# One core, a fused attention and feed-forward kernel: attention inputs stored as whole blocks, the first loads reordered, and two pools moved

## The chip, the cores and the metric

The kernel runs on one core of a Trainium2 chip. The metric is device time in microseconds (us), as the median over runs.

Engines are named as the profile names them. PE is the matmul engine, PEld its weight loads, DVE the vector engine, ACT the scalar (activation) engine, and POOL the GpSimd engine. SP is the engine that issues most transfers here; "SPq" is its queue of instructions. A "DMA share" is the mean busy share of the core's 16 DMA engines.

## The reference, cut to what matters

```python
xn = _layernorm(x)                      # x: 1 x 2048 x 1024, bf16
return x + A(xn) + B(xn)

# B: two gated feed-forward steps
h  = gelu(_layernorm(xn) @ w1)          # 1024 -> 1024
hs = shifted_quarters(h) @ w2           # four column groups shifted by rows
x1 = xn + hs
B  = x1 + gelu(_layernorm(x1) @ w3) @ w4   # 1024 -> 3584 -> 1024

# A: attention over segments of 32 rows, 32 heads of 128, 8 memory rows
for s in segments:
    h = concat([mem, xs]);  q, k, v = h @ Wq, h @ Wk, h @ Wv
    o = softmax(mask(q @ k.T)) @ v @ Wo
    mem = o[:8];  out = o[8:]
```

On PE the kernel does this in five stages:

1. **start and w1**: norms of x, transposes, the w1 matmuls; 
2. **w2**; 
3. **w3** (and w4); 
4. **V**: V = xT·Wv for all rows, stored to memory; 
5. **attention**: Q and K projections, scores, outputs and Wo for five blocks of rows.

## The kernel before: the parts that matter

The V phase has eight head groups `hg`. Each makes 4 x 4 PSUM tiles, evicts them alternately on ACT and DVE into a buffer `Vs` (three of them), and stores each full `Vs` from SP. After head group 1, POOL issues sixteen stores of xT, which the attention blocks read back later.

```python
vsp = vctx.enter_context(tc.tile_pool(name="vsp", bufs=3, side="right"))
...
for hg in range(8):
    ...                                     # loads of Wv and Wo, from POOL
    for m4 in range(4):
        Vs = vsp.tile([P, 4, 512], BF16, tag="Vs")
        for j in range(4):
            ps = psum.tile([P, 512], F32, tag="mm", bufs=4)
            for k in range(KT):
                nc.tensor.matmul(ps[:], xT[:, m4 * 4 + j, k, :], wv[:, k, :], ...)   # L569
            if j % 2 == 0:
                nc.scalar.copy(Vs[:, j, :], ps[:])                                   # L571
            else:
                nc.vector.tensor_copy(Vs[:, j, :], ps[:])                            # L573
        nc.sync.dma_start(V_d[...], Vs[:])                                           # L574
    if hg == 1:
        for t in pns:
            nc.gpsimd.memset(t[:], 0.0)
        for n in range(NT):                                                          # NT = 16
            nc.gpsimd.dma_start(xT_d[:, :, n * P:(n + 1) * P], xT[:, n])             # L579
    if hg == 6:
        first_w = [wtile(), wtile()]        # Wq, Wk of the first head group
        ...
vctx.close()
...
qkv = actx.enter_context(tc.tile_pool(name="aqkv", bufs=2))    # QT, KT, V: where vsp was
```

A later block reads its rows of xT in four or five strided pieces, and the rows of memory are copied in beside them:

```python
hTb = early.tile([P, KT, nt, 104], BF16, tag="hTb")
for i in range(nt):
    nc.gpsimd.dma_start(hTb[:, :, i, 0:96], xT_d[:, :, a + 96 * i:a + 96 * (i + 1)])
nc.vector.tensor_copy(hTb[:, :, :, 96:99], MZ[...])
```

The start loads x in tiles of 128 rows and w1 in two halves of 1 MB. DVE does the statistics, the norms and half of the casts of the first tile.

```python
load_x(0)
for c in range(2):
    nc.sync.dma_start(w1_sb[:, :, c * 512:(c + 1) * 512], w1_v[:, :, c * 512:(c + 1) * 512])
    load_x(c + 1)
for n in range(3, 7):
    load_x(n)
...                                         # in norm1(n), n < 4: a quarter of w2
norm_stats(0)
t0 = xn2T_tile()
xn2 = norm2(0, t0, 0)
norm_stats(1, 0)                            # first half of the statistics of tile 1
transposes(xn2, t0, 0, 0)
transposes(xn2, t0, 0, 1, on_dve=True)
norm_stats(1, 1)
```

The intermediate `h3T` of the w3 stage comes from the pool `p3big`, and the last stores of the output are issued by POOL (`nc.gpsimd.dma_start(out_v[...], ot[:])`).

## Time and profile before

Three runs gave 1540.99 us (1538.52 to 1541.14). The profiled run took 1540.65 us, with a span of 1538.9 us. Each stage starts where its first matmul appears in the view of one line's instructions. The lengths follow by subtraction.

| stage of before | us |
|---|---|
| start and w1 (until the first w2 matmul) | 75.4 |
| w2 | 55.3 |
| w3 and w4 | 413.7 |
| V | 227.1 |
| attention, to its last output matmul | 761.0 |
| from there to the end of the span | 6.4 |

The first view is the page's part 1: engine, busy us, share of the span, number of instructions. PE is the limit, so a change helps only where PE idles or runs at half clock, or after PE's last matmul.

```profile
PE 1516.0 (99%) x9870; PEld 810.3 (53%) x9870; DVE 522.2 (34%) x1094; ACT 506.1 (33%) x1154; POOL 192.5 (13%) x272
```

Next the view of waits for PE. Each line says who waited at which line of the kernel, for whom, then us in all, how often, and the longest.

```profile
PE ps L282 <- DVE xn L261: 7.0, 1, 7.0
PE ps L569 <- ACT Vs L571: 4.3, 1, 4.3
PE ps L514 <- ACT h3T L515: 1.1, 1, 1.1
PE ps L638 <- DMA wt<-in_A_Wq_dram: 1.0, 2, 0.7
PE psO L677 <- DMA PT<-Pn: 0.9, 1, 0.9
PE ps L291 <- DVE xnk L270: 0.8, 1, 0.8
PE psS L653 <- ACT KT L644: 0.6, 1, 0.6
...
```

The largest wait after the start sits in the V phase, on ACT. But ACT itself waited, as the view of its waits from 560 to 600 us shows first. The view of three windows then gives, for each stretch: its length, the busy time of each engine, the granted clock, the DMA share and GB/s.

```profile
ACT Vs L571 <- DMA V_scratch<-Vs: 17.5, 2, 10.7
...
```

```profile
core 0: us, PE busy (x) PEld busy (x) DVE busy (x) ACT busy (x) POOL busy (x), PEclk, DMA share, GB/s
545.00:570.00 25.00, 25.00 (x117) 11.34 (x116) 5.09 (x8) 4.00 (x7) 13.86 (x18) 1.00 0.93 324
570.00:600.00 30.00, 25.73 (x113) 11.27 (x112) 4.75 (x7) 3.90 (x7) 7.25 (x9) 0.95 0.98 260
600.00:630.00 30.00, 30.00 (x139) 13.56 (x138) 5.53 (x8) 5.26 (x9) 1.75 (x2) 0.99 0.60 206
...
```

So ACT could not evict because all three `Vs` were still being stored, and the DMA engines were full (0.98) when it happened. The trace's clock record also shows that PE ran at half clock from 597.16 us for 3.41 us, right after the stall; the granted clocks of 0.95 and 0.99 in the last two windows are this.

The timeline has, per line: start, length, engine, line, operation, and in brackets the idle time before it and what ended that.

At the change from V to attention (771.5 us), the timelines show ACT's first QT eviction after 4.89 us of idling. It waited for the last `Vs` store to land.

```profile
775.42 0.33 SPq L623 DMA_DIRECT2D V<-V_scratch  x1
...
776.62 0.95 SPq L723 DMA_DIRECT2D wt<-in_A_Wq_dram  x2
...
```

```profile
775.44 1.31 ACT L646 ACTIVATE QT<-ps 128x403 bf16<-128x403 f32 x3 [4.89 <-DMA V_scratch<-Vs]
...
```

### The profile page before, as it was taken

The page shows a single profiled execution, that of the slowest core. Times are in us where ns is not written, and L with a number is a line of the kernel's source. Part 1 is how long each engine was busy: PE and PEld are TensorE (multiplying, and loading weights), DVE is VectorE, ACT ScalarE, POOL GpSimd, SP SyncE. Part 2 cuts the span into 40 slices and gives each one's busy share as a digit, 9 for nine tenths or more (in the row PEclk, how much of TensorE's full clock was granted, in tenths as well). Part 3 has the DMA queues.
Part 4 walks back from the last instruction along what each step waited for, and adds up shares of the span by engine and source line. Part 5 has one row for each costly group of instructions (what it writes and reads, how often), then busy time and mean ns, then how long its engine had stood idle before and what let it go on. Part 6 is the DMA issues. An engine that isn't in the chain of part 4 may idle for free. (4 is left out here: it accounts for less than half of the span.)

```text
span 1538.9 us, 24379 instructions
## 1 busy us (share of the span) xinstructions
PE 1516.0 (99%) x9870; PEld 810.3 (53%) x9870; DVE 522.2 (34%) x1094; ACT 506.1 (33%) x1154; POOL 192.5 (13%) x272
## 2 busy tenths in 40 slices
PE   7999999999999998999999999999999999999998
PEld 7844444444444443444456645664665555445554
DVE  8284010000200111122135623651564266416641
ACT  5533203103012011111146614650663266326620
POOL 5232020221211241010000011001000200010001
PEclk9999999999999999999999999999999999999999
DMA  7689543452353898542489956992997389728611
GB/s 253 182 224 309 199 154 121 144 185 83 128 168 83 215 275 260 187 130 69 137 218 250 242 133 166 251 234 71 237 239 196 102 218 228 185 75 207 174 45 50
DMA packets 288445, 270.32 MB, mean 176 GB/s; under 512 B 137307, under 2 KB 255216, under 8 KB 288328
## 3 DMA queue, kind: packets, MB, share of 16 engines
q1 hardware_dynamic: 264936, 185.52, 45.5%
q0 software_dynamic: 23392, 83.19, 16.6%
q8 instruction: 79, 1.29, 0.4%
q14 instruction: 38, 0.31, 0.1%
HBM read 190.73 MB, written 46.73 MB: 154 GB/s over the span
## 5 line engine op out<-in xcount | busy, mean ns | idle before, releaser
L638 PE MATMUL ps<-hTb,wt 128*128 128x396 bf16 (+3 forms) x2560 | 509.9, 343 | 1.0 <-DMA wt<-in_A_Wq_dram 1.0
L638 PEld LDWEIGHTS <-wt 128*128 128x128 bf16 x2560 | 233.9, 97 | 168.3 <-DMA wt<-in_A_Wq_dram 1.8
L569 PE MATMUL ps<-wt,xT 128*128 128x512 bf16 x1024 | 223.0, 381 | 4.3 <-ACT Vs L571 4.3
L696 PE MATMUL pso<-wo_sb,oX 128*128 128x512 bf16 x1024 | 225.1, 379 | 0.0
L514 PE MATMUL ps<-xn3T,w_sb 128*128 128x512 bf16 x896 | 195.9, 379 | 1.1 <-ACT h3T L515 1.1
L539 PE MATMUL ps<-w_sb,h3T 128*128 128x512 bf16 x896 | 195.7, 379 | 0.0
L569 PEld LDWEIGHTS <-xT 128*128 128x128 bf16 x1024 | 100.6, 98 | 126.6 <-issue 6.8
L515 ACT ACTIVATE h3T<-ps 128x512 bf16<-128x512 f32 x112 | 66.5, 597 | 292.0 <-PE ps L514 289.0
L696 PEld LDWEIGHTS <-oX 128*128 128x128 bf16 x1024 | 98.8, 98 | 115.4
L644 ACT CAST KT<-ps 128x396 bf16<-128x396 f32 (+3 forms) x160 | 82.0, 513 | 221.8 <-PE ps L638 219.9
L514 PEld LDWEIGHTS <-w_sb 128*128 128x128 bf16 x896 | 86.7, 98 | 104.0 <-issue 1.3
L539 PEld LDWEIGHTS <-h3T 128*128 128x128 bf16 x896 | 86.8, 98 | 102.8
L659 DVE TENSOR_REDUCE sums<-sm 99x4 f32<-99x396 f32 (+2 forms) x176 | 97.5, 554 | 113.2 <-ACT sm L657 113.2
L655 DVE TENSOR_TENSOR sm<-psS,c_mask_reg_sb 99x396 f32<-99x396 f32 x160 | 91.1, 570 | 88.9 <-PE psS L653 88.4
L657 ACT ACTIVATE sm<-sm 99x396 f32<-99x396 f32 (+2 forms) x176 | 92.7, 527 | 76.3 <-DVE sm L655 75.7
L571 ACT CAST Vs<-ps 128x512 bf16<-128x512 f32 x64 | 37.2, 585 | 239.6 <-PE ps L569 161.4
L646 ACT ACTIVATE QT<-ps 128x396 bf16<-128x396 f32 (+3 forms) x160 | 83.8, 525 | 74.9 <-PE ps L638 50.2
L573 DVE CAST Vs<-ps 128x512 bf16<-128x512 f32 x64 | 44.1, 691 | 183.0 <-PE ps L569 159.3
L665 DVE TENSOR_TENSOR Pn<-sm,rs 99x396 bf16<-99x396 f32 (+2 forms) x176 | 98.9, 562 | 6.2 <-DMA PT<-Pn 0.2
L540 DVE TENSOR_TENSOR R<-ps,R 128x512 f32<-128x512 f32 x32 | 22.1, 691 | 231.8 <-PE ps L539 226.2
L703 POOL DMA_DIRECT2D out_dram<-ot x32 | 17.5, 546 | 588.1 <-DVE ot L702 582.2
L678 ACT CAST oX<-psO 128x384 bf16<-128x384 f32 (+1 forms) x176 | 82.5, 469 | 9.0 <-PE psO L677 8.5
(114 smaller groups left out, 980.8 us busy)
## 6 DMA issues: line engine op xcount, KB each, us to landing
wt<-in_A_Wq_dram SPq DMA_DIRECT2D x78, 512.0 KB
wt<-in_A_Wk_dram SPq DMA_DIRECT2D x78, 512.0 KB
wt<-in_A_Wv_dram POOLq DMA_DIRECT2D x24, 1024.0 KB, 7.0
V_scratch<-Vs SPq DMA_DIRECT2D x32, 512.0 KB
V<-V_scratch SPq DMA_DIRECT2D x32, 384.0 KB
w_sb<-in_B_w_dram SPq DMA_DIRECT2D x9, 1024.0 KB
R_scratch<-x POOLq DMA_DIRECT2D x16, 512.0 KB, 4.3
R<-R_scratch SPq DMA_DIRECT2D x16, 512.0 KB
```

The source lines that it names most:

```text
L514: nc.tensor.matmul(ps[:].rearrange("p (n t) -> p n t", t=P), w3_sb[:, k, f * P:(f + 1) * P], xn3T[tb][:, :, k, :], start=(k == 0), stop=(k ...
L539: nc.tensor.matmul(ps[:], h3T[:, f, j * P:(j + 1) * P], w4_sb[:, f, ch * 512:(ch + 1) * 512], start=(f == 0), stop=(f == FT - 1))
L569: nc.tensor.matmul(ps[:], xT[:, m4 * 4 + j, k, :], wv[:, k, :], start=(k == 0), stop=(k == KT - 1))
L638: nc.tensor.matmul(ps[:, :nb] if flat else ps[:, :nb].rearrange("p (t c) -> p t c", t=nt), w[:, k, hh * P:(hh + 1) * P], B["rhs"](k), star ...
L644: nc.scalar.copy(o, i)
L646: nc.scalar.mul(o, i, scale)
L655: nc.vector.tensor_tensor(sm[:T, :, :T], S3, t["mask"][:].unsqueeze(1).to_broadcast((T, 4, T)), op=ALU.add)
L657: nc.scalar.activation(e[:T, :, :T], sm[:T, :, :T], ACTF.Exp, scale=LN2)
L659: nc.vector.tensor_reduce(ss, e[:T, :, :T], axis=AX.X, op=ALU.add)
L665: nc.vector.tensor_tensor(Pn[:T, :, :T], e[:T, :, :T], rs[:T, :].unsqueeze(2).to_broadcast((T, 4, T)), op=ALU.mult)
L678: nc.scalar.copy(oX[:, hs_, at:at + nt], O3[:, :, 0:nt])
L696: nc.tensor.matmul(self.ps[:], self.oX[:, h, self.gl * P:(self.gl + 1) * P], wo_sb[:, h, self.cc], start=(h == 0), stop=(h == H - 1))
```

## The change

Its intent, part by part:

- **Whole blocks.** In head groups 1 to 4, DVE copies the rows of one attention block, memory rows included, into a tile `hTs`. One contiguous store per block (0.85 to 1.06 MB) replaces the burst of sixteen, and one contiguous load later replaces four or five strided ones.
- **Start.** x's second tile is loaded ahead of w1, w2 is loaded at once, thirteen matmuls on zeros keep PE busy so that its clock opens, the gelu function table is loaded by a dummy activation, and half of tile 1's statistics go into DVE's wait for POOL.
- **Pools.** `h3T` gets a pool of its own; the QT, KT and V pool moves to the other side, away from `vsp`.
- **Small things.** The second head group's Wq is loaded during the V phase, the exp table is loaded there too, and the last two output stores are issued by SP.

```diff
-    xT_d = tc.dram_tile([P, KT, S], BF16, name="xT_scratch")
+    hT_d = {b: tc.dram_tile([P, KT * c], BF16, ...) for b, c in ((1, 416), (2, 416), (3, 432), (4, 520))}
@@ start
                     load_x(0)
+                    load_x(1)
                     for c in range(2):
                         nc.sync.dma_start(w1_sb[:, :, c * 512:(c + 1) * 512], ...)
-                        load_x(c + 1)
-                    for n in range(3, 7):
+                        load_x(c + 2)
+                    for n in range(4, 7):
                         load_x(n)
+                    for i in range(4):
+                        nc.sync.dma_start(w2_sb[:, 2 * i:2 * i + 2, :], ...)
+                    wz = big.tile([P, 512], BF16)
+                    nc.vector.memset(wz[:], 0.0)
+                    gtab = big.tile([P, 1], F32)
+                    nc.scalar.activation(gtab[:], ones_f[:], ACTF.Gelu_apprx_tanh)
+                    ps = psum.tile([P, 512], F32, tag="mm", bufs=4, name="warm")
+                    for i in range(13):
+                        nc.tensor.matmul(ps[:], wz[:, :P], wz[:], start=(i == 0), stop=(i == 12))
                     norm_stats(0)
+                    norm_stats(1, 0)
                     t0 = xn2T_tile()
                     xn2 = norm2(0, t0, 0)
-                    norm_stats(1, 0)
@@ w3 stage
+                h3T = p3.enter_context(tc.tile_pool(name="p3h", bufs=1)).tile([P, FT, 512], BF16)
                 big = p3.enter_context(tc.tile_pool(name="p3big", bufs=1))
...
-                h3T = big.tile([P, FT, 512], BF16)
@@ V phase
+                            if (hg, m4, j) == (7, 3, 2):
+                                nc.scalar.activation(etab[:], ps[:, 0:1], ACTF.Exp, scale=0.0)
...
-                    for n in range(NT):
-                        nc.gpsimd.dma_start(xT_d[:, :, n * P:(n + 1) * P], xT[:, n])
+                if 1 <= hg < 5:
+                    b, (tl, nb) = hg, tiles_of(hg)
...
+                    hTs = abig.tile([P, KT, 432 if b == 3 else 104 * len(tl)], BF16, tag="oX", ...)
+                    nc.gpsimd.memset(hTs[:], 0.0)
+                    fill(hTs, tl, lambda j, b=b: xT[:, j])
+                    nc.gpsimd.dma_start(hT_d[b][:], hTs[:].rearrange("p k c -> p (k c)"))
...
+                if hg == 7:
+                    second_w = [wtile()]
+                    nc.sync.dma_start(second_w[0][:], Wq_v[:, :, 512:1024])
@@ attention
-        qkv = actx.enter_context(tc.tile_pool(name="aqkv", bufs=2))
+        qkv = actx.enter_context(tc.tile_pool(name="aqkv", bufs=2, side="right"))
...                                          # blocks: one load of hTb from hT_d[b]
-                    nc.gpsimd.dma_start(out_v[:, self.gi, self.cc], ot[:])
+                    (nc.sync if self.last else nc.gpsimd).dma_start(out_v[:, self.gi, self.cc], ot[:])
```

More of the change, by code (lines that the diff above doesn't have):

```diff
@@ L112 @@
     xn_v = xn_d.rearrange("(n p) d -> p n d", p=P)
-    xT_d = tc.dram_tile([P, KT, S], BF16, name="xT_scratch")
+    hT_d = {b: tc.dram_tile([P, KT * c], BF16, name=f"hT{b}_scratch") for b, c in ((1, 416), (2, 416), (3, 432), (4, 520))}
     V_d = tc.dram_tile([S, H * DH], BF16, name="V_scratch")
@@ L172, in fill @@
         for t in tl:
-            a = t["tok"]
+            a = 96 * t["gi"]
             end = a + t["ntok"]
@@ L177, in fill @@
                 w = min(P - o, end - a)
-                d = t["c0"] + a - t["tok"]
+                d = t["c0"] + a - 96 * t["gi"]
                 nc.vector.tensor_copy(hTb[:, :, d:d + w], x_of(j)[:, :, o:o + w])
@@ L228 @@
                     load_x(0)
+                    load_x(1)
                     for c in range(2):
                         nc.sync.dma_start(w1_sb[:, :, c * 512:(c + 1) * 512], w1_v[:, :, c * 512:(c + 1) * 512])
-                        load_x(c + 1)
-                    for n in range(3, 7):
+                        load_x(c + 2)
+                    for n in range(4, 7):
                         load_x(n)
+                    for i in range(4):
+                        nc.sync.dma_start(w2_sb[:, 2 * i:2 * i + 2, :], w2_v[:, 2 * i:2 * i + 2, :])
                     stats = {}
@@ L272, in norm1 @@
                         load_x(n + 7)
-                        if n < 4:
-                            nc.sync.dma_start(w2_sb[:, 2 * n:2 * n + 2, :], w2_v[:, 2 * n:2 * n + 2, :])
-                        elif n in (12, 15):
+                        if n in (12, 15):
                             load_w3()
@@ L554 @@
             oT_m = abig.tile([P, H, NQ + 1], BF16)
+            etab = abig.tile([P, 1], F32)
             wo_sb = abig.tile([P, H, D], BF16)
@@ L577 @@
                         nc.gpsimd.memset(t[:], 0.0)
-                    for n in range(NT):
-                        nc.gpsimd.dma_start(xT_d[:, :, n * P:(n + 1) * P], xT[:, n])
+                if 1 <= hg < 5:
+                    b, (tl, nb) = hg, tiles_of(hg)
+                    if b != 3:
+                        for t in tl:
+                            t["c0"] = 104 * t["i"]
+                    hTs = abig.tile([P, KT, 432 if b == 3 else 104 * len(tl)], BF16, tag="oX", name=f"hTs{b}")
+                    nc.gpsimd.memset(hTs[:], 0.0)
+                    fill(hTs, tl, lambda j, b=b: xT[:, j])
+                    nc.gpsimd.dma_start(hT_d[b][:], hTs[:].rearrange("p k c -> p (k c)"))
                 if hg == 6:
@@ L597, in block_setup @@
             ntok = sum(t["ntok"] for t in tl)
-            a = 384 * b
             if b == 0:
                 hTb, rhs = hTb0, lambda k: hTb0[:, k, :nb]
-            elif b == 3:
-                hTb = early.tile([P, KT, 432], BF16, tag="hTb")
-                for t in tl:
-                    nc.gpsimd.dma_start(hTb[:, :, t["c0"]:t["c0"] + t["ntok"]], xT_d[:, :, 96 * t["gi"]:96 * t["gi"] + t["ntok"]])
-                    d = t["c0"] + t["ntok"]
-                    nc.vector.tensor_copy(hTb[:, :, d:d + t["nm"]], MZ[:, :, t["r0"]:t["r0"] + t["nm"]])
-                rhs = lambda k: hTb[:, k, :nb]
             else:
                 nt = len(tl)
-                hTb = early.tile([P, KT, nt, 104], BF16, tag="hTb")
-                r0 = tl[0]["r0"]
-                for i in range(nt):
-                    nc.gpsimd.dma_start(hTb[:, :, i, 0:96], xT_d[:, :, a + 96 * i:a + 96 * (i + 1)])
-                nc.vector.tensor_copy(hTb[:, :, :, 96:99], MZ[:, :, r0:r0 + 3 * nt].rearrange("p k (t r) -> p k t r", t=nt))
-                rhs = lambda k: hTb[:, k, :, 0:99]
-                for i, t in enumerate(tl):
-                    t["c0"] = 104 * i
+                hTb = early.tile([P, KT, 432 if b == 3 else 104 * nt], BF16, tag="hTb")
+                nc.gpsimd.dma_start(hTb[:].rearrange("p k c -> p (k c)"), hT_d[b][:])
+                if b == 3:
+                    rhs = lambda k: hTb[:, k, :nb]
+                else:
+                    rhs = lambda k: hTb[:, k, :].rearrange("p (t c) -> p t c", t=nt)[:, :, 0:99]
+                    for t in tl:
+                        t["c0"] = 104 * t["i"]
             return dict(b=b, tiles=tl, nb=nb, ntok=ntok, rhs=rhs, cols=nb if b in (0, 3) else 104 * len(tl))
@@ L686, in __init__ @@
                 self.oX, self.gi, self.gl, self.cc, self.ps = oX, gi, gl, slice(ch * 512, (ch + 1) * 512), None
-                self.late = False
+                self.late = self.last = False
             def piece(self, hg):
@@ L714, in load_some, with stage_loads @@
                 loads.pop(0)()
-        def stage_loads(Bs, hg, ready=None):
+        def stage_loads(Bs, hg, ready=()):
             cs_ = slice(hg * 512, (hg + 1) * 512)
-            wq, wk = ready or (wtile(), wtile())
+            ws = [(w, None) for w in ready]
+            ws += [(wtile(), src) for src in (Wq_v, Wk_v)[len(ready):]]
+            (wq, _), (wk, _) = ws
             Vs = [qkv.tile([P, len(B["tiles"]), 512], BF16, tag="V", bufs=3, name=f"V{B['b']}") for B in Bs]
-            for w, src in () if ready else ((wq, Wq_v), (wk, Wk_v)):
+            for w, src in ws[len(ready):]:
                 for k0 in (0, 4):
@@ L761 @@
                 if hg < 7:
-                    ahead = stage_loads(Bs, hg + 1)
+                    ahead = stage_loads(Bs, hg + 1, second_w if (gi_, hg) == (0, 0) else ())
                 if hg == 7 and gi_ + 1 < len(groups):
@@ L800 @@
             o.late = True
+        for o in rest[-2:]:
+            o.last = True
         for p in range(6):
```

## The prediction

> **What bounds the kernel now.** PE: the table of busy time gives it 1516.0 of 1538.9 us, in dense runs of matmuls. Only PE's idle time and time at half clock can be won. The view of PE's waits lists about 17 us: 7.0 us at the start (first transpose, waiting for DVE), 4.27 us once in the V phase (waiting for ACT's eviction into Vs), 1.07 us at the start of the w3 stage (ACT's h3T), 0.34 + 0.65 us for the second Wq load, 0.91 us for a PT transpose, 0.81 us at 18 us for a normalized tile, the rest 0.2 to 0.6 each. After PE's last matmul (about 1532.9 us in the timeline) come 6 us of tail.
>
> **Change by change.**
>
> 1. *xT stores.* In the V phase POOL stores xT in 16 pieces of 256 KB (559 to 580 us); the DMA share of 570 to 600 us is 0.98, against 0.52 to 0.60 later. Stores of Vs land late, ACT and DVE wait about 10 us for Vs buffers (until 596.5), and PE stalls 4.27 us. The granted clock then is 0.5 for 3.41 us: another 1.7 us. (The Trainium skill, "TensorE: Matmul & The Clock Gate", section "The HAM clock gate", says an idle window of about 3.4 us halves the clock; the trace agrees.) After: four contiguous stores of 0.85 to 1.06 MB, 27 us apart; I estimate a DMA share of 0.7. Stall and half clock go: **-6.0 us**. DVE pays with 9 to 12 copies per block, 0.18 to 0.36 us each by hTb's copies in the trace: bursts of about 2.6 us against one PSUM bank of four filled per 1.73 us. That barely fits: +0.3 us.
>
> 2. *Start.* PE's first 40 matmuls take about 112 ns each, later ones 65. Thirteen zero matmuls in the idle 7 us should leave the clock full at 7.0 us. The gelu table load (1.28 us at 8.24 us) leaves the chain; half of tile 1's statistics fills DVE's 0.85 us wait for POOL. First transpose still near 7.0 us; the second tile's near 11.0 instead of 12.04 us. From there to 18 us DVE paces the stage, and its chain gains only about 0.8 us: **-0.8 us**, not the 2 to 3 us that the clock suggests. w2 at once fills a gap of the DMA (13 to 19 us); nothing waits for it now: 0.
>
> 3. *h3T's pool*: its first eviction no longer waits for the last xn3 transposes: **-1.1 us**.
>
> 4. *Second Wq loaded in the V phase*: **-1.0 us**. QT no longer waits 4.9 us for the last Vs store, but PE never waited for that: 0. The exp table load: 0.
>
> 5. *Last two stores from SP*: tail **-0.7 us** (estimate from POOL's 0.54 us issue, the wait before it and the flag's load).
>
> 6. One hTb load per block in place of 18 strided ones: off the path; PT's 0.91 us may shrink: **-0.3 us**.
>
> Sum -9.6 us.
>
> **Prediction: 1532 us, 80% range 1528 to 1537.** Chances: faster by over 2% 0.01, within 2% 0.98, slower by over 2% 0.01.
>
> **Right if**: no PE wait above 1 us in the V phase and granted clock 1.0 from 590 to 605 us; the h3T and Wq waits gone; second tile's transposes at 10.5 to 11.5 us; PE's busy time grows by the zero matmuls only.
>
> **Wrong if**: the zero matmuls end before the clock opens, or w1's first half lands after 8 us because tile 1 precedes it; DVE bursts stall V evictions; Wk now comes late in Wq's place; QT's place over xT makes evictions wait for the last V matmuls.

## More of the kernel before

DVE runs without a gap from 11.14 us until it writes `xnk`, which the first segment sums wait for. This `xnk` belongs to tile 0 of x, whose statistics DVE did from 3.58 us on; it comes so late because the program lets DVE do the statistics of tiles 3 and 4 first.

```profile
11.14 0.55 DVE L261 TENSOR_SCALAR xn<-xt,mv,rr 128x1024 bf16<-128x1024 bf16 x1 [0.81 <-POOL rr L253]
...
13.47 0.68 DVE L246 BATCH_NORM_STATS2 st<-xt 128x6 f32<-128x512 bf16 x1
...
17.68 0.54 DVE L270 TENSOR_SCALAR xnk<-xt,mv,rr 128x1024 bf16<-128x1024 bf16 x1
...
```

## The result, and the profile after

Six runs of each kernel: 1530.13 us after (1529.11 to 1531.21) against 1540.04 us before (1537.76 to 1541.14). The ratio is 0.9938 with a 95% interval of 0.9925 to 0.9951. A ratio is the mean time of one kernel's runs over the mean of the other's runs of the same rounds, so it isn't quite the ratio of the medians. The gain is under 2%, and the interval shows that there is a gain. The profiled run of after took 1529.11 us, with a span of 1527.2 us. It is the fastest of its six, so the two profiled runs lie 11.5 us apart where the medians lie 9.9 us apart.

The stage table splits the 11.7 us between the two profiled spans:

| stage | before | after | difference | predicted |
|---|---|---|---|---|
| start and w1 | 75.4 | 75.1 | -0.3 | -0.8 |
| w2 | 55.3 | 55.0 | -0.3 | 0 |
| w3 and w4 | 413.7 | 412.5 | -1.2 | -1.1 |
| V | 227.1 | 221.0 | -6.1 | -6.0 + 0.3 |
| attention | 761.0 | 758.1 | -2.9 | -1.0 - 0.3 |
| last output matmul to the end | 6.4 | 5.5 | -0.9 | -0.7 |

PE's busy time in after's page is a little low, because the trace lacks some matmul records (1004 of 1024 in the V stage), so idle time is read from the waits and stage starts instead. The view of PE's waits in after, whole:

```profile
PE ps L300 <- DMA w_sb<-in_B_w_dram: 2.0, 1, 2.0
PE ps L283 <- DVE xn L264: 1.3, 1, 1.3
PE warm L317 <- DVE wz L311: 1.3, 1, 1.3
PE ps L292 <- DVE xnk L273: 0.7, 1, 0.7
PE ps L300 <- ACT xn2T L287: 0.2, 1, 0.2
PE pso L710 <- issue: 0.2, 1, 0.2
```

The waits in the V phase, at `h3T`, for Wq, for PT and for KT are gone. One wait is new: 2.0 us for the first half of w1. The windows of the V phase in after:

```profile
core 0: us, PE busy (x) PEld busy (x) DVE busy (x) ACT busy (x) POOL busy (x), PEclk, DMA share, GB/s
545.00:570.00 25.00, 24.89 (x116) 11.33 (x117) 6.38 (x17) 4.59 (x8) 8.41 (x9) 1.00 0.90 328
570.00:600.00 30.00, 29.84 (x138) 13.58 (x140) 7.77 (x19) 4.89 (x9) 6.94 (x6) 1.00 0.61 207
600.00:630.00 30.00, 29.84 (x138) 13.62 (x140) 7.98 (x21) 5.07 (x9) 7.70 (x6) 1.00 0.67 228
...
```

From 570 to 600 us the DMA share fell from 0.98 to 0.61, and the clock is 1.00. ACT's waits from 560 to 600 us are now for PE alone:

```profile
ACT Vs L581 <- PE ps L579: 34.5, 12, 2.9
```

DVE at the start of after: the second tile's norm comes 0.80 us earlier than before (10.34 against 11.14), but then DVE idles 0.80 us for tile 3 of x, and `xnk`, which stands behind tile 3's statistics in DVE's program, is no earlier than it was.

```profile
10.34 0.55 DVE L264 TENSOR_SCALAR xn<-xt,mv,rr 128x1024 bf16<-128x1024 bf16 x1 [0.82 <-POOL rr L256]
...
13.56 0.69 DVE L249 BATCH_NORM_STATS2 st<-xt 128x6 f32<-128x512 bf16 x1 [0.80 <-DMA xt<-in_A_x_dram]
...
17.77 0.54 DVE L273 TENSOR_SCALAR xnk<-xt,mv,rr 128x1024 bf16<-128x1024 bf16 x1
...
```

At the change from V to attention (763.6 us in after) the first load of V starts at 765.54, 1.9 us after the stage and not 3.9, and ACT's first QT eviction idles 1.02 us, not 4.89:

```profile
765.54 1.14 SPq L637 DMA_DIRECT2D V<-V_scratch  x1
...
```

```profile
765.15 0.51 ACT L660 ACTIVATE QT<-ps 128x403 bf16<-128x403 f32 x1 [1.02 <-PE ps L652]
...
```

### The profile page after: what moved, and what is told of

It reads as the page before. It is cut to its first block, busy times and chain, and to the rows that moved or that the text cites. A ratio compares the mean times of both kernels' runs of the same rounds, so it can differ in the third digit from the quotient of the medians.

```text
span 1527.2 us, 24314 instructions
## 1 busy us (share of the span) xinstructions
PE 1512.6 (99%) x9810; PEld 810.3 (53%) x9883; DVE 530.1 (35%) x1131; ACT 506.8 (33%) x1155; POOL 178.8 (12%) x248
## 4 chain that ended last, share of the span: by engine, by line
PE 98%; DMA 1%; DVE 0%; issue 0%; ACT 0%; SPq 0%
PE ps L652 30%; PE ps L579 14%; PE pso L710 14%; PE ps L523 13%; PE ps L548 13%; PE ps L387 4%; PE ps L300 3%; PE psS L667 2%; PE psO L691 2%; DMA xt<-in_A_x_dram 1%; PE ps L474 1%; PE ps L837 1%; PE ps L440 1%; PE gps L454 1%; PE ps L292 0%
## 5 line engine op out<-in xcount | busy, mean ns | idle before, releaser
L549 DVE TENSOR_TENSOR R<-ps,R 128x512 f32<-128x512 f32 x32 | 22.1, 692 | 232.0 <-PE ps L548 221.1
```

## The experiments

The main theory was the prediction's: the burst of stores is worth 6 us, and the rest is small. The rivals were that the strided form of the stores, and not their burst, did the harm; that the start gains nothing; and that the attention gain comes from the pool's place, not from the early Wq. Twelve runs were made, eleven of other kernels and one of the changed kernel again, all with correct results. The table collects what they showed; "w1" is the time of the first w1 matmul, "sums" that of the first segment sums, "tail" the time from PE's end to the end of the span.

| run | w1 | sums | V stage | attention | tail | POOL's drain |
|---|---|---|---|---|---|---|
| before | 8.3 | 18.3 | 227.1 | 761.0 | 6.0 | 3.17 |
| before_hts | 8.3 | 18.3 | 221.0 | 760.8 | 8.5 | 5.87 |
| before_spread | 8.2 | 18.5 | 221.0 | 760.7 | 6.0 | 3.17 |
| hts_sp | 8.4 | 18.4 | 221.0 | 762.1 | 7.8 | 5.21 |
| start_only | 10.0 | 18.8 | 225.8 | 761.6 | 6.0 | 3.17 |
| after | 9.5 | 18.4 | 221.0 | 758.1 | 5.1 | hidden |
| after_again | 9.7 | 18.6 | 221.0 | 758.6 | 5.9 | hidden |
| tail_undone | 10.2 | 19.0 | 221.0 | 757.9 | 8.5 | 5.87 |
| small_undone | 10.5 | 19.6 | 221.1 | 758.6 | 4.9 | hidden |
| old_order | 8.1 | 18.4 | 221.0 | 757.9 | 5.4 | hidden |
| no_warm | 10.2 | 19.1 | 221.0 | 758.1 | 5.2 | hidden |
| qkv_left | 9.8 | 18.7 | 221.0 | 762.1 | 5.2 | hidden |
| w1_split | 7.9 | 18.4 | 221.0 | 757.9 | 5.3 | hidden |
| start_best | 8.1 | 18.6 | 221.0 | 762.0 | 5.0 | hidden |

"Hidden" means that no long drain of POOL follows PE's last matmul: POOL's last work is done earlier, and SP stores the last output. The drain is there in all eight, and takes 5.70 us.

### before_hts: the whole-block stores and loads alone

```diff
 # kernel before, with only hT_d, fill, hTs and the single load of hTb from the change
-                    for n in range(NT):
-                        nc.gpsimd.dma_start(xT_d[:, :, n * P:(n + 1) * P], xT[:, n])
+                if 1 <= hg < 5:
+                    ...
+                    fill(hTs, tl, lambda j, b=b: xT[:, j])
+                    nc.gpsimd.dma_start(hT_d[b][:], hTs[:].rearrange("p k c -> p (k c)"))
```

> The kernel before with the block inputs alone changed (laid out in the V phase, stored whole, loaded whole); start, pools, weights and tail as before. Theory: the 4.27 us stall of PE in the V phase comes from the 16 xT stores, so it goes with them, and with it 3.41 us at half clock: 6.0 us faster, a ratio of about 0.9961, no PE wait above 1 us between 545 and 770 us, clock 1.0 there. Rival: the stall is the other traffic of that stretch (Wo, Wv, Vs) or the old places of the pools: a stall of at least 2 us stays, ratio above 0.998.

Measured: 1538.32 us (1537.74 to 1539.07, 4 runs) against 1540.19 for before (7 runs), ratio 0.9993 (0.9976 to 1.0009). The stall and the half clock are gone and the V stage is 6.1 us shorter, as expected. Yet the whole time hardly moved: the expected ratio of 0.9961 was missed, and 0.9993 can't be told from no change. The profile shows 2.4 us of the loss at the end, where POOL's drain, an instruction after its last store, grew from 3.17 to 5.87 us. The start was 1.1 us longer (w2 begins at 76.5), with a wait of 1.3 us for a transposed tile that before's profile doesn't have. PE's waits for Wq grew from 1.0 to 1.6 us. So in the profiles the V stage's gain is real and was partly lost at the tail; this profile's run is 2.9 us faster than before's, and where the rest of the gain went in the other runs isn't shown.

### before_spread: the old form of stores, without the burst

```diff
-                if hg == 1:
-                    ...
-                    for n in range(NT):
+                if 1 <= hg < 5:
+                    for n in range(4 * hg - 4, 4 * hg):
                         nc.gpsimd.dma_start(xT_d[:, :, n * P:(n + 1) * P], xT[:, n])
```

> The kernel before, its 16 xT stores unchanged in form, but four each in four head groups in place of sixteen in one. Theory A (it was the burst: 4.2 MB in 21 us on top of Wo, Wv and Vs): stall and half clock go as in the run with whole blocks, 6.0 us faster, ratio about 0.9961. Theory B (it was the form: 16 strided stores, each partition in eight 256-byte pieces): the stall stays in part, PE waits 2 us or more in the V phase, ratio above 0.998.

Measured: 1534.91 us (1533.69 to 1536.40), ratio 0.9970 (0.9954 to 0.9987). The V stage took 221.0 us, exactly as with whole blocks, with no wait of PE in it. The windows of this run, to be read against before's second one:

```profile
570.00:600.00 30.00, 29.84 (x137) 13.60 (x139) 5.53 (x8) 5.28 (x9) 5.28 (x6) 1.00 0.65 219
...
```

The waits for Wq (1.3 us), h3T (1.1 us) and PT (0.5 us) are left. Sixteen strided stores of 256 KB do no harm when four go out at a time, so the burst was needed for the stall. (Whole blocks in one burst were not run, so whether the form alone would have helped isn't shown.) The whole-block form adds nothing to the V stage, and DVE's copies for it (7.77 us of DVE in the window after, against 4.75 before) cost PE nothing.

### start_only: the start's part of the change alone

The edit is the diff's part "start" on the kernel before, with nothing else.

> The kernel before with the start alone changed (x tiles 0 and 1 first, w2 at once, half of tile 1's statistics early, gelu table early, zero matmuls). Theory from the changed kernel's trace: w1's first half now lands late, PE waits about 2 us for it near 7.5 us, the clock falls to a half again at about 11 us, and the segment sums of tile 0 run at 18.3 to 18.4 us as before: gain at that point 0. Rival (the late landing was chance of one run): the wait is under 0.5 us, the second tile's transposes run near 11.0 us, the segment sums near 17.5 us. The V-phase stall of 4.3 us stays either way.

Measured, one look: 1539.86 us, against 1540.19 for before in its rounds. The first w1 matmul is at 10.0 us instead of 8.3, the segment sums at 18.8 instead of 18.3, w2 at 75.5 instead of 75.4. The start shows no gain by itself. The V stall is there, 3.4 us in this run.

### after_again: the changed kernel once more

> The changed kernel once more, for a second profile. If the order of the loads makes w1's first half late, PE again waits 1.5 to 2.5 us for it; if the slow landing was chance, under 0.5 us. No V-phase stall; second Wq and h3T waits absent.

Measured: 1530.65 us. The w1 wait came again (2.1 us, then 1.0 us), the waits in the w3, V and attention stages did not, but for 0.2 us for PT. The two profiles of this kernel differ by 0.2 us in the segment sums, 0.5 us in the attention stage and 0.9 us in the tail. At the start the spread is wider: in the six profiles with exactly after's start the segment sums are at 18.4 to 19.6 us and w2 at 75.1 to 76.7 us.

### tail_undone: the last two stores back on POOL

```diff
         for o in rest[-2:]:
-            o.last = True
+            o.last = False
```

> The changed kernel with the last two output stores issued by POOL again. In the run with whole blocks alone, POOL's closing drain took 5.87 us after its last store (3.17 us in the kernel before), and 8.5 us passed from PE's last matmul to the end (6.0 before, 5.1 and 5.9 in the two profiles of the changed kernel). Theory: whole-block transfers lengthen that drain, so here the tail is again about 8.5 us and the time 2.5 to 3.5 us above the changed kernel's, near 1533; the stores from SP are worth that, not 0.7 us. Rival: the long drain was chance; tail 6.0 us, time within 1 us of the changed kernel's.

Measured: 1533.63 us (1532.82 to 1534.27), ratio 0.9954 (0.9937 to 0.9971), against 0.9938 for the change. The drain is 5.87 us, as in before_hts, and the tail 8.5 us. So storing from SP is worth 2.6 to 3.6 us in this kernel's tail (8.5 less 4.9 to 5.9), as the whole-block version made the drain longer. The ratios give 2.5 us, with intervals that overlap. Against before, the two effects nearly cancel.

### small_undone: h3T back in its old pool, and no early second Wq

```diff
-                h3T = p3.enter_context(tc.tile_pool(name="p3h", bufs=1)).tile([P, FT, 512], BF16)
...
+                h3T = big.tile([P, FT, 512], BF16)
...
-                if hg == 7:
-                    second_w = [wtile()]
-                    nc.sync.dma_start(second_w[0][:], Wq_v[:, :, 512:1024])
```

> The changed kernel with h3T back in its old pool and the second Wq loaded in attention again. Theory: the two waits come back where they were: 1.07 us for h3T at the start of the w3 stage and 1.0 to 1.6 us for Wq in the second head group; stretch from the first attention projection to the last output matmul longer by the second amount, so from 758.1 to about 759.5 us. If it rises to 761 us as before, the early Wq is worth also the later waits for PT and KT. Rival: other changes (QT's place, hTb loads) removed them; no wait comes back.

Measured: 1532.24 us. The h3T wait is back, and the Wq wait is not:

```profile
PE ps L300 <- DMA w_sb<-in_B_w_dram: 3.0, 1, 3.0
...
PE ps L523 <- ACT h3T L524: 1.1, 1, 1.1
PE psO L688 <- DMA PT<-Pn: 0.5, 1, 0.5
...
```

The h3T term stands at 1.1 us. (Another 1.6 us of this run's time is its start: w2 is at 76.7 us, with 3.0 us of waiting for w1.) The early second Wq isn't needed to remove the Wq wait: without it the attention stage is still 758.6 us long. With the pool in its new place SP issues this load 3.3 us into the stage, where in before it did so after 5.1 us (776.62):

```profile
769.84 0.95 SPq L736 DMA_DIRECT2D wt<-in_A_Wq_dram  x2
...
```

### old_order: the load order of before, with the rest of the change

```diff
                     load_x(0)
-                    load_x(1)
                     for c in range(2):
...
-                        load_x(c + 2)
+                        load_x(c + 1)
...                                         # and tile 1's first statistics after norm2(0)
```

> The changed kernel with the loads of x and w1 in the old order (tile 1 after w1's first half) and tile 1's first half of statistics after the first normalization; zero matmuls, early gelu table and w2 at once stay. Theory: w1's first half lands before 8 us, PE's first w1 matmul starts at 7.9 to 8.1 us at full clock with no wait above 0.5 us for w1, and tile 0's segment sums run by 17.7 us, 0.7 us earlier than now, as DVE paces that point; the w2 stage starts near 74.5 instead of 75.1 to 75.3 us. Rival: zero matmuls on PE themselves slow the loads: w1 still lands after 9 us.

Measured: 1529.18 us. The first w1 matmul is at 8.1 us and w1's matmuls until 14 us take 219 ns each (median), against 311 ns in before, so the clock is full. PE has both things that the start was meant to give. But the segment sums are at 18.4 us and w2 at 75.1 us, and the expectation (17.7 and 74.5) fell: PE now waits for DVE instead. Its waits at the start are 0.8 us and 1.8 us for DVE's casts and norms, and DVE's chain runs as in before (the second tile's norm at 11.27 us, `xnk` at 17.81).

### no_warm: without the matmuls on zeros

```diff
-                    ps = psum.tile([P, 512], F32, tag="mm", bufs=4, name="warm")
-                    for i in range(13):
-                        nc.tensor.matmul(ps[:], wz[:, :P], wz[:], start=(i == 0), stop=(i == 12))
```

> The changed kernel without the 13 zero matmuls. Theory: PE waits for w1 until 9.5 to 10 us in any case and the first matmuls merely run at half clock: w2 stage starts within 0.5 us of the changed kernel's (75.1 to 75.3 us), segment sums of tile 0 at 18.4 to 19 us. Rival 1: zero matmuls slow the loads, then w1 lands before 8.5 us here. Rival 2: they are worth 1 us or more at the w2 stage.

Measured: 1530.85 us. w1 is as late as in after (10.2 us), so the zero matmuls don't cause that. The segment sums are at 19.1 us and w2 at 76.7 us, against 75.1 to 75.3 in the two profiles of the change. But small_undone, which has the zero matmuls, also starts w2 at 76.7 us, and 0.7 us here is a wait for a transposed tile. So one profile doesn't show what the zero matmuls are worth, or that they are worth anything.

### qkv_left: the QT, KT and V pool back over vsp

```diff
-        qkv = actx.enter_context(tc.tile_pool(name="aqkv", bufs=2, side="right"))
+        qkv = actx.enter_context(tc.tile_pool(name="aqkv", bufs=2))
```

> The changed kernel with the QT, KT and V pool back on the left side, over the V phase's buffers; the early second Wq load is kept. Theory A (the pool's place delays the first V load, and everything queued behind it): the first attention load of V starts only after the last store of Vs has landed, 3.5 to 5 us after the attention stage began instead of about 1.4 us; ACT's first QT eviction waits 4 to 5 us; the second Wq load isn't queued there any more, so no Wq wait; but later loads are late, and PT or KT waits of 0.3 to 0.9 us come back; attention stage 759.0 to 760.5 us from its first projection to its last matmul stage, against 758.1 to 758.6. Theory B (QT's wait never reaches PE, as predicted): attention stays at 758.0 to 758.6 us. One time about 1530 to 1532 us.

Measured: 1533.42 us. It was run on another chip. The first load of V starts at 768.20, 4.3 us after the stage began (763.9). Three fences follow: SP's waits around the change of stage in before, the same view in this run, and PE's waits in this run from 763 to 900 us, whole.

```profile
SPq L623 <- DMA V_scratch<-Vs: 2.2, 1, 2.2
...
```

```profile
SPq L637 <- DMA V_scratch<-Vs: 2.2, 1, 2.2
...
```

```profile
PE psO L691 <- DMA PT<-Pn: 3.1, 4, 1.4
PE ps L652 <- DMA wt<-in_A_Wq_dram: 0.2, 1, 0.2
```

The same wait of 2.2 us for the last `Vs` store is in both. The attention stage took 762.1 us, outside the range that either theory gave, but on theory A's side. The early Wq is still there, and PE's wait for Wq is 0.2 us. The lost time comes as four waits for transposed P tiles (PT). Theory A says that they follow from what was queued behind the late V load, but SP's timeline speaks against that. Below is SP in this run, and then in after, whose stage begins 0.3 us earlier: 11 us into the stage, and at the first PT transpose, SP is level in both. The listed waits for PT begin only 43 us into the stage, at 806.72 us.

```profile
774.60 0.40 SPq L739 DMA_DIRECT2D wt<-in_A_Wq_dram  x1
779.32 1.21 SPq L682 DMA_TRANSPOSE PT<-Pn  x1
...
```

```profile
774.33 0.40 SPq L739 DMA_DIRECT2D wt<-in_A_Wq_dram  x1
779.01 1.21 SPq L682 DMA_TRANSPOSE PT<-Pn  x1
...
```

So the cause of these 3.1 us stays open.

### w1_split: the first half of w1 in two pieces

```diff
-                    for c in range(2):
-                        nc.sync.dma_start(w1_sb[:, :, c * 512:(c + 1) * 512], ...)
-                        load_x(c + 2)
-                    for n in range(4, 7):
+                    nc.sync.dma_start(w1_sb[:, :, 0:256], w1_v[:, :, 0:256])
+                    nc.sync.dma_start(w1_sb[:, :, 256:512], w1_v[:, :, 256:512])
+                    load_x(2)
+                    nc.sync.dma_start(w1_sb[:, :, 512:1024], w1_v[:, :, 512:1024])
+                    for n in range(3, 7):
                         load_x(n)
```

> The changed kernel with the first half of w1 loaded as two pieces of 256 columns ahead of tile 2, the second half after it. Theory A (the size of the first piece makes the first w1 matmul late): the first piece lands before 8.2 us, PE's wait for it falls from 2.0 to under 0.5 us, the clock stays full after the zero matmuls, the segment sums of tile 0 begin at 17.4 to 17.9 us instead of 18.4. Theory B (DVE's norms and transposes pace the start, as the run with the old order suggested): the wait for w1 goes but the segment sums stay at 18.2 to 18.6 us. Whole time within 0.8 us of the changed kernel's 1530.1.

Measured: 1529.06 us. It was run on another chip. The first w1 matmul is at 7.9 us and the clock stays full. The segment sums are at 18.4 us and w2 at 75.1 us, as in the change. Theory A falls: its wait for w1's first half is gone, and the sums are no earlier. The late first half alone isn't what holds the start back. (PE still waits 1.4 us for w1, now for the second half.) DVE's timeline has the same two facts as in after: it idles for tile 3 of x, and `xnk` comes at 17.80.

```profile
13.59 0.69 DVE L250 BATCH_NORM_STATS2 st<-xt 128x6 f32<-128x512 bf16 x1 [0.84 <-DMA xt<-in_A_x_dram]
...
17.80 0.54 DVE L274 TENSOR_SCALAR xnk<-xt,mv,rr 128x1024 bf16<-128x1024 bf16 x1
...
```

### start_best: the same, and DVE freed of its cast

```diff
 # as w1_split, and
-                    transposes(xn2, t0, 0, 0)
-                    transposes(xn2, t0, 0, 1, on_dve=True)
                     norm_stats(1, 1)
+                    transposes(xn2, t0, 0, 0)
+                    transposes(xn2, t0, 0, 1)
```

> As the run with w1 in pieces, and both casts of the first tile's transposes moved from DVE and ACT to ACT alone, behind the statistics of tile 1's second half on DVE. Theory B (DVE paces the start): with DVE freed, the second tile's transposes begin at 10.2 to 11.2 us instead of 11.9, segment sums at 16.5 to 17.6 us, the w2 stage at 73.3 to 74.4 instead of 75.1, whole time 1528.6 to 1529.8 us, ratio to before 0.9925 to 0.9935. Theory A (w1 alone paces it): no better than the run with w1 in pieces alone, ratio 0.994. If ACT becomes the next limit, the transposes of the second tile stay at 11.5 us or later.

Measured: 1530.65 us (1529.12 to 1534.89, 4 runs), ratio 0.9931 (0.9914 to 0.9948), which can't be told from the change's 0.9938. It was run on another chip. The second tile's norm moved up to 8.94 us and its transposes to 10.9 us, as theory B said. Nothing came of it: DVE now idles twice for x, and `xnk` is at 18.03 us. In this profile w2 begins at 77.2 us, where 73.3 to 74.4 was expected; after the sums PE waits 1.6 us for transposed tiles.

```profile
8.94 0.54 DVE L265 TENSOR_SCALAR xn<-xt,mv,rr 128x1024 bf16<-128x1024 bf16 x1 [0.82 <-POOL rr L257]
10.47 0.70 DVE L250 BATCH_NORM_STATS2 st<-xt 128x6 f32<-128x512 bf16 x1 [0.98 <-DMA xt<-in_A_x_dram]
...
13.81 0.70 DVE L250 BATCH_NORM_STATS2 st<-xt 128x6 f32<-128x512 bf16 x1 [1.38 <-DMA xt<-in_A_x_dram]
...
18.03 0.54 DVE L274 TENSOR_SCALAR xnk<-xt,mv,rr 128x1024 bf16<-128x1024 bf16 x1
...
```

So neither theory named the limit. In both profiles the chain hangs on the landing of tile 3 of x, at 13.59 us in w1_split and 13.81 us here: `xnk` follows 4.2 us later, after the statistics of tiles 3 and 4. Yet tile 0's `xnk` needs neither tile. No run moved it ahead of them in DVE's program, so what that would bring isn't shown; PE's wait for it is 0.8 us. This run's profile is its slowest (1534.89 us), and its attention stage has 2.4 us of PT waits and 0.8 us of Wq waits although the pool is on the new side and V is loaded 2.0 us into the stage:

```profile
PE psO L692 <- DMA PT<-Pn: 2.4, 3, 1.2
```

So such waits come with the new place too, and their cause stays open.

### hts_sp: the whole-block transfers issued by SP

```diff
 # before_hts, and
-                    nc.gpsimd.dma_start(hT_d[b][:], hTs[:].rearrange("p k c -> p (k c)"))
+                    nc.sync.dma_start(hT_d[b][:], hTs[:].rearrange("p k c -> p (k c)"))
-                nc.gpsimd.dma_start(hTb[:].rearrange("p k c -> p (k c)"), hT_d[b][:])
+                nc.sync.dma_start(hTb[:].rearrange("p k c -> p (k c)"), hT_d[b][:])
```

> The kernel before with the whole-block stores and loads alone (as the first run), but both issued by SP in place of POOL; the last two output stores stay on POOL. Theory A (the whole-block transfers on POOL's queue lengthen its drain at the end): drain 3.2 us or less, time from PE's last matmul to the end about 6.0 us or less. Theory B (the drain's length comes from something else, such as fewer transfers on POOL's queue): drain stays near 5.9 us, tail near 8.5. The V stage stays free of PE's stall in both (about 221 us long); the attention stage keeps its waits (pool on the left), 760.5 us or more.

Measured: 1536.86 us (the one run of before beside it took 1550.81, so no ratio is made of it). It was run on another chip. The drain is 5.21 us although POOL issues none of the whole-block transfers. Theory A falls, and what makes the drain 3.17, 5.21 or 5.87 us stays open.

## Why the prediction was right, and where it wasn't

The predicted 1532 us lies within 2 us of the 1530.13 measured, and 1530.13 is inside the range of 1528 to 1537. The predicted sum was -9.6 us; the medians differ by 9.9 us. The V stage carries most of it and was predicted for the right reason. That the sum came so close is partly luck: in the profiles the start gave 0.5 us less than predicted and the attention stage 1.6 us more, and the tail's two errors cancelled. Point by point:

1. **The stall in the V phase: right, in cause and size.** Predicted -6.0 + 0.3, measured -6.1 us (227.1 to 221.0). The chain was: sixteen stores from POOL fill the DMA engines, the `Vs` stores from SP land late, no `Vs` buffer is free, ACT can't evict, PE stops for 4.27 us and then runs 3.41 us at half clock, which costs half of that. before_spread shows that it took the burst. The Trainium skill, "DMA: Bandwidth & Descriptors", section "Issuing engines are not separate DMA queues", says that transfers issued by different engines run on the same 16 DMA engines; the trace agrees, with POOL's stores delaying SP's at a share of 0.98. The feared stall from DVE's bursts of copies didn't come: no PE wait in the V stage in any of the eleven profiles with whole blocks.

2. **The start: wrong; this is the step that failed.** The prediction said "From there to 18 us DVE paces the stage, and its chain gains only about 0.8 us: -0.8 us". DVE's chain did gain that 0.80 us up to the second tile's norm, and lost 0.80 us again to tile 3 of x, which in before had been there when DVE got to it. The segment sums stand at 18.4 us against 18.3. The windows from 4 to 7 us show why it landed later: with x's second tile ahead of w1, the DMA moved 190 to 266 GB/s in all nine profiles with the new order (222 in after), with the old order 344 to 374 in all five. The zero matmuls and the early w2 don't explain it: old_order has both at 344 GB/s, and no_warm has no zero matmuls at 190. So what stands behind it, w1's first half and tile 3, came later. The prediction's list of what would make it wrong has a part of this, "w1's first half lands after 8 us because tile 1 precedes it". It does (9.5 us), but in w1_split mending it brought the sums no earlier. And with the old order DVE's chain gains nothing, so old_order isn't better either. The second tile's transposes, predicted at 10.5 to 11.5 us, came at 11.86 in after, behind the late w1 matmuls, during which the clock had halved (at 10.77 us). The stage's own -0.3 us is less than the spread between profiles (w2 at 74.9 to 76.5 us in the four profiles with before's start). Why the DMA is slow with the new order is open.

3. **h3T's pool: right.** Predicted -1.1, measured 1.1 us of wait removed, and back again in small_undone.

4. **The second Wq: its wait went, but not by this alone; most of the stage's gain is unexplained.** The prediction gave -1.0 us to the early load, 0 to QT's place and 0.3 to the hTb loads, 1.3 us in all for the attention stage, which gained 2.9. Either move removes the wait for Wq: small_undone takes the early Wq away and no Wq wait returns; qkv_left takes the new place away and 0.2 us of it is left. With the old place SP must wait for the last `Vs` store before it may load V, and in before the Wq load stood behind that in SP's queue. So "PE never waited for that: 0" was a mistake: PE did not wait for QT's eviction, but in before it waited 1.0 us for Wq, which the same release had held back. The rest of the gain goes with the pool's place in most profiles, without a shown cause: all six with the old place have an attention stage of 760.7 to 762.1 us, seven of the eight with the new place 757.9 to 758.6 us, and the eighth, start_best, 762.0. qkv_left is the only run that changes the place alone, in one profile, and there SP was level again long before the PT waits. The hTb loads show no gain: with the old place the stage is 760.8 and 762.1 us with whole loads, 760.7 to 761.6 with strided ones. Of the 2.9 us, the listed waits account for 2.3 (2.5 us in before less 0.2 in after).

5. **The tail: the net was near (-0.9 against -0.7), the terms were mis-sized.** The stores from SP are worth 2.6 to 3.6 us in the tail, not 0.7, because the whole-block version came with a longer drain on POOL, which alone costs 2.4 us (before_hts). With both, the tail is 4.9 to 5.9 us where it was 6.0, so a net of 0.1 to 1.1 us. The prediction had not looked at the drain at all, and that its net came out is luck.

6. **The function tables: right for exp in that the trace has no PE wait on it, untested alone.** In before the exp table load (1.28 us) sits between an eviction and the first exp, at 785.85 us; in after it runs from 762.66 to 763.94 us, at the change from V to attention. No run isolates it, so a part of the attention stage's 2.9 us could be its.

No version tried beats the changed kernel by more than the runs' spread (w1_split ran on another chip): old_order and w1_split had 1529.18 and 1529.06 us in one run each, within 0.1 us of the lower end of the change's own range (1529.11 to 1531.21).

## What to carry to other kernels

When transfers from several engines share the DMA engines, spread a large side job over the stage in which it runs before changing its form: here four strided stores at a time gave the whole 6.1 us. When an engine off the critical path waits for a buffer, follow what else stands in the same queue behind that wait, because PE may feel it there: here it was the Wq load, and 1.0 us. And before counting a faster start as a gain, check when the last input that the stage needs will land; here DVE's chain gained 0.80 us in front of a late transfer and lost it there. Look as well at the order of the engine's program, as work that needs nothing late can stand behind work that does.

## What the Trainium skill lacked or had wrong

- "TensorE: Matmul & The Clock Gate", "The HAM clock gate": the half-rate state lasts 3.41 us in before, as the page's window has it. The page ties it to an idle window. In after the clock halved at 10.77 us although PE had worked about 1.4 of the 3.41 us before that (idle from 7.51 to 9.55 us), and in qkv_left at 11.11 us after about 1.3 us of work. In after_again, with the same code and nearly the same gaps, it did not halve. The page says that the window's phase varies by run, which agrees; it doesn't say how much work a window may hold and still halve the clock.
- "DMA: Bandwidth & Descriptors", "Rules for kernel authors": the page advises merging small transfers, and counts those under 64 KB as small. Merging 256 KB stores, which are above that, into 0.85 to 1.06 MB brought nothing here beyond spreading them (V stage 221.0 us both ways, with no PE wait left in it). The page doesn't name bursts.
- No page says what the order of the first loads does to the rate: 190 to 266 GB/s from 4 to 7 us with two 256 KB tiles ahead of w1, 344 to 374 GB/s with one.
- "ScalarE: Activation LUTs", "What ACT_TABLE_LOAD costs": the load takes 1.28 us, as the page says (about 1283 ns). The drain of about 1380 ns that it adds isn't seen: before's exp table load starts at 785.85 us, right after an eviction of 0.51 us from 785.32, and the next activation at 787.14.
- No page has a drain of POOL this long at the end of a kernel: 3.17 us in before, before_spread and start_only, 5.87 us in before_hts and tail_undone, 5.21 us in hts_sp, 5.70 us in the other eight.
